# A gated mix of a Fourier convolution and a bilinear unit on one core: three Fourier stages on sums and differences of their inputs

## The chip, the core and the metric

The kernel runs on one core of a Trainium2 chip. The core's engines work side by side, each through its own queue in order: TensorE (PE) multiplies matrices, with its weight loads listed as PEld, VectorE (DVE) and ScalarE (ACT) work on tiles, GpSimd (POOL) and SyncE (SP) issue DMAs. Matmul results go to PSUM, here eight banks of 128 x 512 floats. The metric is the device time of one execution in microseconds; of several runs the median counts. The span is the stretch of the profiled execution from its first to its last instruction.

## What is computed

The input u has 2048 tokens and 512 channels. One branch convolves every channel with a kernel K of 2048 taps, which is itself made from 128 complex modes per channel; the other is a bilinear unit with hidden width 1792. A gate per token mixes them.

```python
P = jnp.exp((A * dt[:, None])[:, :, None] * pos[None, None, :])
K = 2.0 * jnp.einsum("dn,dnl->dl", C, P).real
Kf = jnp.fft.rfft(K, L2)
Uf = jnp.fft.rfft(u_t, L2)
y = jnp.fft.irfft(Uf * Kf[None, :, :], L2)[:, :, :L]
a = y.T + u * D_skip
b = ((x @ w_gate) * (x @ w_up)) @ w_down
g = sigmoid((u * gate_w).sum(-1))
out = g * a + (1 - g) * b
```

Here L2 is 4096, and x of the bilinear unit is read from u as well.

## The kernel before

**The order.** The kernel's work is written as tasks (`add`): an engine, an estimated time, what it reads and writes, a rank and, for some, an earliest time. `Work.run` then plays them on a clock of its own: it starts at each step the task that can start soonest, the lower rank first among equals, and emits the instructions in that order. On the chip only the resulting order of each engine's queue is left; nothing waits for the planner's clock.

**The bilinear unit (GLU).** The hidden width is cut into 14 tiles in five groups, and the tokens into four blocks of 512, which gives 56 calls of `hidden`, each of 24 matmuls for the gate (`pg`) and up (`pu`) products; `down` adds 672 more into `y`. Every float is split in a high and a low part (`xhi`, `xlo`, `whi`, `wlo`, `hh`, `hl`, `dhi`, `dlo`) and three products are summed, so the GLU is 2016 matmuls of 128x128 by 128x512. ScalarE makes the high parts and VectorE the low ones. Call number n of `hidden` may not start before `T_STEP * n - 5` on the planner's clock. GLU matmuls have rank 2, the highest number: Fourier work goes ahead of them where both can start. Group results are added into the output in DRAM by accumulating DMAs on GpSimd's queue (`out<-acc`); the last block of the last group is summed in the tile `kt` in `ends`.

**The tables and K.** For each of 16 blocks of 32 channels, `phases`, `amplitudes`, `direct_powers`, `leads`, `x_table` and `v_table` build two tables of powers, x (32 entries) and v (64 entries), on VectorE and ScalarE. `k_block` multiplies them on TensorE (`k<-v,x`) into one bank: 32 by 64 taps per channel. ScalarE copies that bank into `kt`, transposed, 32 elements apart. The last piece of a v table is the second `v<-v,sq` of its block.

**The Fourier transform.** A transform of 4096 points is done as a first stage over 64 points (`k_first` for K, in `u_part` for u), a second over 32 points (`m_second`), the product of the two spectra (`m_product`), an inverse (`m_inverse`) and a last stage (`m_last`). They run for four quarters q of 128 channels, each after the four blocks of K that it needs; a quarter's second stage is four tiles T. Between stages the data turn around in DRAM: `su_d` (u after its first stage), `sk_d` (K after its first), `y_d` (after the inverse). All these matmuls are in plain float32, in parts of the array (`tile_position`): u's first stage as two halves of 64 rows, the second stage as 64x32 tiles, the inverse as 32x64, the last as 128x64. The four small PSUM banks that they share are called `k`, as is K's own; so a Fourier batch reads `k<-in,w_t` (u's first or the last stage), `k<-kt,w1k_t` (K's first), `k<-in,w2s`, `k<-x,w2s` or `k<-v,w2s` (second) and `k<-y,w3s` (inverse). Batches of transforms are kept 6 us apart on the planner's clock (`APART`), in the last quarter 4 us (`LESS`). In the last quarter copies out of PSUM alternate between ScalarE and VectorE (`evict`).

## Time and profile before

| | before |
|---|---|
| median of 3 runs | 618.17 us (617.34 to 620.17) |
| span of the profiled execution | 615.6 us |
| instructions | 17,970 |
| granted TensorE clock, mean | 0.999 |
| PE / DVE / ACT / POOL busy | 605.5 / 514.9 / 420.1 / 88.6 us |
| moved by DMA | 121.67 MB, mean 198 GB/s |
| packets under 2 KB, of all | 66,548 of 103,238 |

A row of the profile's groups reads: line, engine, operation, tile written <- tiles read, shapes, count, then busy time and the mean of one in ns, then the idle time of the engine ahead of them and what ended it. All lines are L100 since one helper issues everything, so the tiles tell the groups apart. A row of the timeline has its start in us, the length of the stretch, the engine and the count. A float32 matmul stands twice in the trace, so `x128` there are 64 matmuls of the program. Recorded times of neighbours overlap by a few hundredths, on TensorE by more; the price of an instruction in a stream is the distance from start to start.

### The profile page before, as it was taken

What the parts mean: (1) busy time and instruction counts of PE and PEld (TensorE: products, weight loads), DVE (VectorE), ACT (ScalarE), POOL (GpSimd) and SP (SyncE); (2) the same over time, 40 slices, a digit from 0 to 9 for tenths busy, and PEclk for the clock granted to TensorE, in tenths of its full rate; (3) what the DMA queues carried; (4) which work ended last, traced back from release to release, by engine and by line L of the source; (5) the groups of instructions that cost most, each with busy time, mean ns of one, the idle gap of its engine ahead of it and who ended that gap; (6) DMA issues with size and microseconds to landing.
All of it is one profiled execution on the core that took longest, in us unless ns stands there. A gap on an engine that the chain in (4) does not pass through costs nothing.

```text
span 615.6 us, 17970 instructions
## 1 busy us (share of the span) xinstructions
PE 605.5 (98%) x7524; PEld 468.9 (76%) x7524; DVE 514.9 (84%) x810; ACT 420.1 (68%) x953; POOL 88.6 (14%) x125
## 2 busy tenths in 40 slices
PE   8999999999999999999999999999999999999996
PEld 5776777788777788887768888786888887678865
DVE  6958999999999999999889999999999842377342
ACT  5469877896878886679688768878885663533320
POOL 0211111111112201010120202021110101210120
PEclk9999999999999999999999999999999999999999
DMA  8795736555677977748797939787996789897771
GB/s 284 221 283 181 242 111 199 171 180 119 158 198 189 234 206 191 172 121 206 245 229 181 235 112 229 221 239 167 196 237 194 188 232 308 205 278 199 170 107 69
DMA packets 103238, 121.67 MB, mean 198 GB/s; under 512 B 6644, under 2 KB 66548, under 8 KB 102900
## 3 DMA queue, kind: packets, MB, share of 16 engines
q1 hardware_dynamic: 83732, 92.33, 49.3%
q0 software_dynamic: 19008, 28.06, 25.4%
q8 instruction: 59, 0.97, 0.6%
q14 instruction: 23, 0.19, 0.1%
q10 hardware_dynamic: 416, 0.13, 0.1%
HBM read 69.37 MB, written 51.12 MB: 196 GB/s over the span
## 4 chain that ended last, share of the span: by engine, by line
PE 75%; issue 10%; DMA 7%; DVE 4%; ACT 3%; POOL 1%; POOLq 0%; ACTq 0%; DVEq 0%
PE pg L100 20%; PE y L100 19%; PE pu L100 19%; PE k L100 18%; DMA out<-acc 3%; DMA raw<-in_xT 3%; ACT acc L100 1%; ACT ts L100 1%; DMA y<-in_xT 1%; DVE xlo L100 1%; POOL out L100 1%; ACT rt L100 1%; POOL su_d L100 1%; DVE v L100 1%; DVE t L100 1%
## 5 line engine op out<-in xcount | busy, mean ns | idle before, releaser
L100 POOL DMA_DIRECT2D out<-acc x60 | 51.3, 891 | 369.1 <-ACT acc L100 327.2
L100 PE MATMUL y<-dhi,hl 128*128 128x512 f32 x224 | 90.7, 405 | 1.5 <-ACT acc L100 0.9
L100 PE MATMUL pg<-xhi,wlo 128*128 128x512 f32 x224 | 90.3, 403 | 0.4 <-ACT h L100 0.3
L100 PE MATMUL pg<-xlo,whi 128*128 128x512 f32 x224 | 87.8, 392 | 1.6 <-issue 1.2
L100 PE MATMUL pu<-xhi,wlo 128*128 128x512 f32 x224 | 89.3, 399 | 0.0
L100 PE MATMUL pg<-xhi,whi 128*128 128x512 f32 x224 | 87.7, 392 | 0.5 <-ACT whi L100 0.5
L100 PE MATMUL y<-dhi,hh 128*128 128x512 f32 x224 | 87.5, 390 | 0.0
L100 PE MATMUL y<-dlo,hh 128*128 128x512 f32 x224 | 87.4, 390 | 0.0
L100 PE MATMUL pu<-xhi,whi 128*128 128x512 f32 x224 | 87.4, 390 | 0.0
L100 PE MATMUL pu<-xlo,whi 128*128 128x512 f32 x224 | 87.4, 390 | 0.0
L100 ACT ACTIVATE acc<-y,ngate 128x512 f32<-128x512 f32 x76 | 51.8, 692 | 29.9 <-PE y L100 18.4
L100 DVE TENSOR_TENSOR h<-pu,h 128x512 f32<-128x512 f32 x56 | 38.5, 688 | 39.7 <-PE pu L100 39.4
L100 ACT CAST hh<-h 128x512 fp32r<-128x512 f32 x56 | 34.9, 623 | 38.3 <-DVE h L100 38.2
L100 ACT COPY ts<-k 128x512 f32<-128x512 f32 (+1 forms) x112 | 47.7, 503 | 13.8 <-PE k L100 13.7
L100 PEld LDWEIGHTS y<-dhi,hl 128*128 128x128 f32 x224 | 42.0, 188 | 18.6 <-issue 2.7
L100 PEld LDWEIGHTS pg<-xhi,wlo 128*128 128x128 f32 x224 | 42.1, 188 | 18.1 <-issue 7.8
L100 ACT COPY h<-pg 128x512 f32<-128x512 f32 x56 | 32.9, 588 | 30.7 <-PE pg L100 24.5
L100 PEld LDWEIGHTS pu<-xhi,wlo 128*128 128x128 f32 x224 | 42.0, 188 | 12.7 <-issue 3.0
L100 PEld LDWEIGHTS pg<-xhi,whi 128*128 128x128 f32 x224 | 42.1, 188 | 12.5 <-ACT whi L100 2.1
L100 PEld LDWEIGHTS y<-dhi,hh 128*128 128x128 f32 x224 | 42.0, 188 | 9.3
L100 PEld LDWEIGHTS pu<-xhi,whi 128*128 128x128 f32 x224 | 42.2, 188 | 9.0
L100 PEld LDWEIGHTS pg<-xlo,whi 128*128 128x128 f32 x224 | 42.2, 188 | 8.8 <-DVE xlo L100 0.7
(109 smaller groups left out, 1169.5 us busy)
## 6 DMA issues: line engine op xcount, KB each, us to landing
raw<-in_xT SPq DMA_DIRECT2D x60, 256.0 KB, 4.6
out<-acc POOLq DMA_DIRECT2D x60, 256.0 KB, 6.7
raw<-in_wts SPq DMA_DIRECT2D x36, 256.0 KB, 4.4
su_d<-ts POOLq DMA_DIRECT2D x32, 256.0 KB, 4.6
y_d<-ts SPq DMA_DIRECT2D x16, 512.0 KB, 4.7
sk_d<-ts SPq DMA_DIRECT2D x14, 512.0 KB, 5.3
in<-sk_d SPq DMA_DIRECT2D x12, 512.0 KB, 6.8
in<-su_d SPq DMA_DIRECT2D x12, 512.0 KB, 5.4
```

What stands on the lines that cost most here:

```text
L100: got = getattr(self.engine, name)(*args, **kw)
```

## The change

The points of the transform are taken about the middle of the sequence. Tokens n1 and 63 - n1, and n2 and 31 - n2, are added and subtracted first, so cosines meet only sums and sines only differences, and each matrix has half its rows or columns:

- **u's first stage.** `u_part` now takes four columns of tokens at a time, four times instead of eight. VectorE makes two wide and four narrow sums and differences; then two batches of eight matmuls run in 32x64 tiles over 512 columns, where four matmuls in 64x128 halves ran per part. `su_d` is written in runs of 2 KB.
- **K.** Its powers lie in another order in v. ScalarE copies half of a bank into `kt` in reverse, and VectorE writes sum and difference of the halves. K's first stage has the same number of columns in one piece. `sk_d` is written in runs of 4 KB instead of 512 B.
- **The second stage** takes u and K side by side as 256 columns, in sixteen 32x32 tiles: 32 matmuls for both in a tile T, where 64 of 128 columns ran before. The product writes over its input tile.
- **The last stage** runs in 64x32 tiles on even and odd halves apart; ScalarE copies the odd half, VectorE adds and subtracts, and only then the gate multiplies. `y_d` is read in runs of 8 KB.
- **The steps**: `T_STEP` 9.85 instead of 10.3, and u's parts at 9, 29, 49 and 69 on the planner's clock instead of every 15.

```diff
-T_STEP = 10.3
+T_STEP = 9.85
+U_STEP = 20.0
...
-    def u_part(c):
...
+    def u_part(t):
+        ut = inp([P, 4, D])
+        rs = slice(4 * t, 4 * t + 4)
+        add("sp", 0.42, lambda: sp.dma_start(ut.t, uv[:, rs, :]), w=[ut], dma=1024, after=9.0 + U_STEP * t)
...
-        banks = [[bank() for _ in range(2)] for _ in range(2)]
-        sts = [stage([P, 2, D]) for _ in range(2)]
-
-        def fn():
-            for j in range(2):
-                for h in range(2):
-                    half = slice(64 * h, 64 * h + 64)
-                    pe.matmul(
-                        banks[j][h].t, w1_t[half], ut.t[half, j, :], start=True, stop=True, tile_position=(64 * h, 0)
-                    )
-
-        for j in range(2):
...
+        ones = [new("mid", "y", [P, 2, D], bufs=2) for _ in range(2)]
+        ops = (ALU.add, ALU.subtract)
+        for y, op in zip(ones, ops):
+            add(
+                "dve", 1.22,
+                lambda y=y, op=op: dve.tensor_tensor(out=y.t, in0=ut.t[:, :2], in1=ut.t[:, 2:], op=op), r=[ut], w=[y],
+            )
+        for s, op in enumerate(ops):
+            for d, y in enumerate(ones):
+                add(
+                    "dve", 0.69,
+                    lambda d=d, s=s, y=y, op=op: dve.tensor_tensor(
+                        out=ut.t[:, 2 * s + d], in0=y.t[:, 0], in1=y.t[:, 1], op=op
+                    ),
+                    r=[y], w=[(ut, 2 * s + d)],
+                )
+
+        def first(s):
+            banks, st = [bank() for _ in range(4)], new("mid", "ev", [P, KT, 4, P], bufs=2)
+
+            def fn():
+                for p in range(2):
+                    col, src = 64 * (p + s), 2 * s + (p + s) % 2
+                    for tq in range(4):
+                        lanes = slice(32 * tq, 32 * tq + 32)
+                        pe.matmul(
+                            banks[tq].t[64 * p : 64 * p + 64], w1_t.t[lanes, col : col + 64], ut.t[lanes, src],
+                            start=True, stop=True, tile_position=(32 * tq, 64 * p),
+                        )
+
+            add("pe", 1.08, fn, r=[(ut, 2 * s), (ut, 2 * s + 1), w1_t], w=banks, rank=1, hold=[st])
+            for tq in range(4):
+                add(
+                    "act", 0.59,
+                    lambda tq=tq: act.copy(st.t[:, :, tq], banks[tq].t.rearrange("p (f d) -> p f d", f=KT)),
+                    r=[banks[tq]], w=[(st, tq)],
+                )
...
+                        su_d[q, :, n0 : n0 + 4, :].rearrange("(t a) n d -> a t (n d)", a=4),
+                        st.t[:, q].rearrange("p n d -> p (n d)"),
...
-        for to, of, n in ((32, 0, 16), (56, 32, 8)):
+        for to, of, n in (((33, 64, 2), (0, 16, 1), 16), ((34, 64, 4), (33, 49, 2), 8)):
...
-            kts["now"] = new("tab", "kt", [P, 64, 32])
+            kts["now"] = new("tab", "kt", [P, 2, 2, 16, 32])
         kt, g0 = kts["now"], b % 4 * 8
         add("pe", 2.15, kgen, r=[x, v], w=[pk], rank=0, hold=[kt], many=work.APART)
-        add(
-            "act", 1.09,
-            lambda: act.copy(
-                kt.t[:, :, g0 : g0 + 8].rearrange("p n g -> p g n"), pk.t.rearrange("p (g j) -> p g j", j=64)
-            ),
-            r=[pk], w=[(kt, b % 4)],
-        )
+        pv = lambda a: pk.t.rearrange("p (g a b k) -> p g a b k", a=2, b=2, k=16)[:, :, a]
+        side = lambda h: kt.t[:, h, :, :, g0 : g0 + 8].rearrange("p b k g -> p g b k")
+        add("act", 0.6, lambda: act.copy(side(1), pv(0)[:, :, :, ::-1]), r=[pk], w=[(kt, (1, b % 4))])
+        for h, op in enumerate((ALU.add, ALU.subtract)):
+            add(
+                "dve", 0.45, lambda h=h, op=op: dve.tensor_tensor(out=side(h), in0=pv(1), in1=side(1), op=op),
+                r=[pk, (kt, (1, b % 4))], w=[(kt, (h, b % 4))], rank=0,
+            )
...
-                to = 0
-                for first, n, second in K_COLS[h]:
-                    for b in range(2):
-                        n0 = (first, second)[b]
-                        for c in range(4):
-                            lanes = slice(32 * c, 32 * c + 32)
-                            pe.matmul(
-                                banks[c].t[:, 32 * to : 32 * (to + n)], w1k_t[lanes, b],
-                                kt.t[lanes, n0 : n0 + n, :].rearrange("p n g -> p (n g)"),
-                                start=b == 0, stop=b == 1, tile_position=(32 * c, 0),
-                            )
-                    to += n
-
-            add("pe", 2.08, fn, r=[kt, m_w1k], w=banks, rank=-1, hold=sts, many=apart_of(q))
+                for b in range(2):
+                    for c in range(4):
+                        lanes = slice(32 * c, 32 * c + 32)
+                        pe.matmul(
+                            banks[c].t, w1k_t[lanes, b, 64 * h : 64 * h + P],
+                            kt.t[lanes, h, b].rearrange("p k g -> p (k g)"),
+                            start=b == 0, stop=b == 1, tile_position=(32 * c, 0),
+                        )
+
+            add("pe", 1.95, fn, r=[kt, m_w1k], w=banks, rank=-1, hold=sts, many=apart_of(q))
...
-                        sk_d[q, :, n0 : n0 + 8, :],
-                        st.t.rearrange("p n c g -> p n (c g)"),
+                        sk_d[q, :, n0 : n0 + 8, :].rearrange("(t a) n d -> a t (n d)", a=4),
+                        st.t.rearrange("p n c g -> p (n c g)"),
...
+            t, at = inp([P, 8, 2, P]), lambda: t.t
+            t = new("tab", "x", [P, 8, 2, P], bufs=2)
+                late["v"] = new("tab", "v", [P, 2, 8, 2, P])
+            t = late["v"]
...
-        banks = [[bank() for _ in range(2)] for _ in range(2)]
-        tos = [new("mid", "ev", [P, 2, 2, 2 * P], bufs=3) for _ in range(2)]
-            for which, (src, k) in enumerate(ins):
-                for part in range(2):
-                    for i in range(2):
-                        for j in range(4):
-                            for e in range(2):
-                                half = slice(64 * e, 64 * e + 64)
-                                c0 = 2 * P * part + P * i
-                                pe.matmul(
-                                    banks[which][e].t[32 * j : 32 * j + 32, c0 : c0 + P],
-                                    w.t[half, 4 * i + j, 32 * part : 32 * part + 32], src.t[half, k, 4 * i + j, :],
-                                    start=True, stop=True, tile_position=(64 * e, 32 * j),
-                                )
-
-        add("pe", 2.13, fn, r=[*ins, w], w=banks[0] + banks[1], rank=1, hold=tos, many=apart_of(q))
+        banks = [bank() for _ in range(4)]
+        to = new("mid", "ev", [P, 2, 2, 2, 2 * P], bufs=2)
+        at, parts = ins
+            src = at()
+            for f in range(8):
+                c, h = f % 4, f // 4
+                for r in range(4):
+                    lanes = slice(32 * r, 32 * r + 32)
+                    pe.matmul(
+                        banks[r].t[32 * c : 32 * c + 32, 2 * P * h : 2 * P * h + 2 * P], w.t[lanes, f],
+                        src[lanes, f].rearrange("p w d -> p (w d)"), start=True, stop=True,
+                        tile_position=(32 * r, 32 * c),
+                    )
+
+        add("pe", 1.15, fn, r=[*parts, w], w=banks, rank=1, hold=[to], many=apart_of(q))
...
-    def m_last(q, halves):
+    def m_last(q, gs):
...
+            for bs, t in zip(banks, src):
+                for tq in range(4):
+                    for p in range(2):
+                        lanes = slice(64 * p, 64 * p + 64)
+                        pe.matmul(
+                            bs[p].t[32 * tq : 32 * tq + 32], w4_t[lanes],
+                            t.t[lanes, 4 * tq : 4 * tq + 4].rearrange("p n d -> p (n d)"), start=True, stop=True,
+                            tile_position=(64 * p, 32 * tq),
+                        )
...
+            even, odd = banks[gs.index(g)]
+            cut = lambda x, n0=n0, n=n: x.t.rearrange("p (t s d) -> p t s d", t=2, s=2)[:, n0 : n0 + n]
+            side = lambda s1, fin=fin: fin.t[:, :, s1]
+            us = 0.15 + 0.27 * n
+            add("act", us - 0.1, lambda cut=cut, odd=odd, side=side: act.copy(side(1), cut(odd)), r=[odd], w=[(fin, 1)])
+            for s1, op in enumerate((ALU.add, ALU.subtract)):
+                add(
+                    "dve", us,
+                    lambda s1=s1, op=op, cut=cut, even=even, side=side: dve.tensor_tensor(
+                        out=side(s1), in0=cut(even), in1=side(1), op=op
+                    ),
+                    r=[even, (fin, 1)], w=[(fin, s1)], rank=0,
+                )
...
+            late["y"] = [new("tab", "x", [P, 16, P], bufs=2) for _ in range(2)]
+            for g in range(2):
+                for half in range(2):
+                    for p in range(2):
+                        lanes = slice(64 * p + 32 * half, 64 * p + 32 * half + 32)
+                        rows_y = y_d[q, 64 * half : 64 * half + 64].rearrange("(k p) n d -> p k (n d)", p=2)
+                        add(
+                            "sp", 0.42,
+                            lambda t=late["y"][g], lanes=lanes, rows_y=rows_y, p=p, g=g: sp.dma_start(
+                                t.t[lanes], rows_y[p, :, 16 * P * g : 16 * P * g + 16 * P]
+                            ),
+                            r=[(m_y, (q, 2 * half + k)) for k in range(2)], w=[(late["y"][g], (half, p))], dma=256,
```

The tables of sines and cosines change with it (`fourier_matrices`), as do the place of each token in the input and output arrays, the number of buffers of two tags (`in` and `ev`, three to two), and the gate's score, which now lies in the gate's own tile.

The change also moves instructions. On TensorE, this is the second stage of the last quarter in the kernel before; `pg`, `pu` and `y` are GLU matmuls:

```order
L100 MATMUL pu<-xlo,whi 128x512
L100 MATMUL pu<-xhi,whi 128x512
L100 MATMUL k<-v,w2s 32x128 x32
L100 MATMUL k<-x,w2s 32x128 x32
L100 MATMUL pu<-xhi,wlo 128x512
L100 MATMUL pu<-xlo,whi 128x512
```

And this is the whole of the last quarter behind K's first stage, in the changed kernel:

```order
L120 MATMUL y<-dlo,hh 128x512
L120 MATMUL y<-dhi,hh 128x512
L120 MATMUL k<-x,w2s 32x256 x64
L120 MATMUL k<-y,w3s 64x128 x64
L120 MATMUL k<-v,w2s 32x256 x64
L120 MATMUL k<-y,w3s 64x128 x64
L120 MATMUL k<-x,w_t 32x512 x16
L120 MATMUL y<-dhi,hl 128x512
```

Before, GLU matmuls stand between the batches, and 75 behind the last; now the batches follow each other and 18 GLU matmuls are behind them. Counted from the last block of K (`k<-v,x`), 357 of the 2016 GLU matmuls stood behind it, and now 108 do.

On VectorE, the end of the last v table in the kernel before:

```order
L100 TENSOR_TENSOR v<-v,sq 128x32x16
L100 TENSOR_TENSOR h<-pu,h 128x512
L100 SCALAR_TENSOR_TENSOR v<-v 128x32x8
L100 TENSOR_TENSOR v<-v,sq 128x32x8
L100 TENSOR_TENSOR hl<-h,hh 128x512
L100 TENSOR_TENSOR xlo<-raw,xhi 128x512 x2
```

and in the changed kernel:

```order
L120 TENSOR_TENSOR hl<-h,hh 128x512
L120 SCALAR_TENSOR_TENSOR v<-v 128x32x16
L120 TENSOR_TENSOR v<-v,sq 128x32x16
L120 SCALAR_TENSOR_TENSOR v<-v 128x32x8
L120 TENSOR_TENSOR xlo<-raw,xhi 128x512
L120 TENSOR_TENSOR v<-v,sq 128x32x8
L120 TENSOR_TENSOR kt<-k,kt 128x8x32 x2
```

Behind that table VectorE had 11 `xlo`, 10 `h` and 11 `hl` left; now it has none, three and three, and the sum and difference of K's last block (`kt<-k,kt`) come right behind the table.

Also on VectorE, the sums and differences of u's first part in the changed kernel (`y<-in`, `in<-y`), which the kernel before does not have:

```order
L120 TENSOR_TENSOR y<-in 128x1024
L120 TENSOR_TENSOR xlo<-raw,xhi 128x512
L120 TENSOR_TENSOR y<-in 128x1024
L120 TENSOR_TENSOR t<-v,turns 128x672
L120 TENSOR_TENSOR in<-y 128x512 x2
L120 TENSOR_TENSOR h<-pu,h 128x512
L120 TENSOR_TENSOR in<-y 128x512
L120 TENSOR_TENSOR xlo<-raw,xhi 128x512
```

They stand among the GLU's low parts and the tables, and u's matmuls wait for them.

More of the change, by code (lines that the diff above doesn't have):

```diff
@@ L351, in gated_mix_kernel @@
     pars = {}
-    gw = new("mid", "bd", [P, D])
+    gw = new("mid", "w3s", [P, D], bufs=2)
+    w1_t = new("mid", "w2s", [P, 192], bufs=2)
     def memsets():
@@ new lines, in u_part @@
+        for s, op in enumerate(ops):
[25 more added lines that the diff above has]
+                )
+            n0 = 16 * s + 4 * t
+            for q in range(KT):
```

346 lines of the change are left out of this document (173 added, 173 removed).

## The prediction

> **What bounds the kernel now.** I read the busy shares first, then one table of windows cut at the points where the Fourier work changes character, then TensorE's timeline at the end. In the windows each row gives the length, then PE, PEld, DVE, ACT and POOL busy, the clock, the DMA share and GB/s.
>
> ```profile
> PE 605.5 (98%) x7524; PEld 468.9 (76%) x7524; DVE 514.9 (84%) x810; ACT 420.1 (68%) x953; POOL 88.6 (14%) x125
> ...
> 0.00:60.00 60.00, 57.34 (x227) 40.67 (x228) 43.86 (x100) 38.92 (x98) 10.09 (x37) 1.00 0.77 244
> 60.00:494.20 434.20, 431.67 (x5900) 339.35 (x5906) 417.07 (x627) 338.52 (x773) 62.21 (x72) 1.00 0.74 192
> 494.20:535.30 41.10, 41.10 (x383) 30.22 (x367) 11.83 (x23) 20.13 (x47) 6.52 (x6) 1.00 0.91 252
> 535.30:589.75 54.45, 54.25 (x947) 43.64 (x946) 32.73 (x47) 20.11 (x34) 6.88 (x8) 1.00 0.90 210
> 589.75:615.60 25.85, 21.17 (x92) 14.98 (x91) 9.36 (x16) 2.42 (x4) 2.87 (x2) 0.99 0.41 78
> ```
>
> VectorE's 84% hides two stages. From 60 to 494.2 us it is busy 417.07 of 434.2 us, 96%: it builds the tables from which K is made, and that queue is full. From 494.2 on it is busy 53.9 of 121.4 us. TensorE is full throughout. So until the last table both engines bound the kernel together, and behind it TensorE alone does. This is TensorE behind that point:
>
> ```profile
> 501.11 2.07 PE L100 MATMUL k<-v,x 128*32 128x64 f32 x128
> ...
> 507.41 2.00 PE L100 MATMUL k<-kt,w1k_t 32*128 32x512 f32 x16
> ...
> 513.65 2.04 PE L100 MATMUL k<-kt,w1k_t 32*128 32x256 f32 x48
> ...
> 535.31 1.16 PE L100 MATMUL k<-v,w2s 64*32 64x128 f32 x64
> 536.21 1.22 PE L100 MATMUL k<-x,w2s 64*32 64x128 f32 x64
> ...
> 571.46 2.15 PE L100 MATMUL k<-y,w3s 32*64 32x128 f32 x128
> ...
> 589.75 3.65 PE L100 MATMUL k<-v,w_t 128*64 128x512 f32 x16
> ```
>
> The last block of K is made at 501.11, its first stage ends at about 515.65, the second stage of the last quarter starts at 535.31, its last stage at 589.75. That chain of 88.6 us is serial through VectorE and DRAM, and today GLU matmuls cover it: by the order 357 of the 2016 stand behind the last block of K.
>
> **The change on TensorE.** Prices are steps from the start of a batch to the start of what follows.
>
> ```profile
> 20.65 1.99 PE L100 MATMUL k<-in,w_t 64*128 64x512 f32 x8
> 22.56 0.50 PE L100 MATMUL pu<-xhi,wlo 128*128 128x512 f32 x1
> ...
> 223.71 2.11 PE L100 MATMUL k<-in,w2s 64*32 64x128 f32 x128
> 225.75 0.50 PE L100 MATMUL y<-dhi,hl 128*128 128x512 f32 x1
> ...
> 309.82 2.79 PE L100 MATMUL k<-in,w_t 128*64 128x512 f32 x12
> 312.44 1.03 PE L100 MATMUL k<-y,w_t 128*64 128x512 f32 x4
> 313.40 0.50 PE L100 MATMUL pg<-xhi,wlo 128*128 128x512 f32 x1
> ...
> 246.65 0.39 PE L100 MATMUL pu<-xhi,wlo 128*128 128x512 f32 x1
> ...
> 248.46 0.39 PE L100 MATMUL pu<-xhi,whi 128*128 128x512 f32 x1
> 248.78 2.10 PE L100 MATMUL k<-y,w3s 32*64 32x128 f32 x128
> 250.81 0.50 PE L100 MATMUL pu<-xhi,wlo 128*128 128x512 f32 x1
> ```
>
> A batch of u takes 1.91 us, a second stage 2.04, a last stage 3.58; a GLU matmul 0.226 (eight steps in 1.81). The inverse batch runs in tiles of 32x64, eight at once: 128 records of 128 columns in 2.03 us, 16,384 columns. u's new batch uses the same tiles with half those columns: 1.0 us. The last stage of a quarter has the same columns: 2.0. The second stage halves its columns only if sixteen 32x32 tiles run at once, which no row shows: between 1.0 (they do) and 2.0 (eight do). I take 1.0, since 64-row and 32-row tiles both reached eight. Saved: 8 x 0.9 + 16 x 1.0 + 4 x 1.6 = 29.6 us in all, and 8 x 0.9 + 12 x 1.0 + 2 x 1.6 = 22.4 ahead of the last block of K. K's first stage keeps its columns; the saving there is nothing or a few hundredths, within the bounds below.
>
> But the order also moves 249 GLU matmuls ahead of that block (357 behind it become 108), 56.3 us. TensorE therefore cannot be there before 501.1 + 56.3 - 22.4 = **535 us**.
>
> **The change on VectorE.** The table's last piece today, the three groups of GLU work that still stand behind it (window from 494.2), those of the same kind ahead of it (from 60), and the prices:
>
> ```profile
> 493.81 0.42 DVE L100 TENSOR_TENSOR v<-v,sq 128x256 f32<-128x256 f32 x1
> ...
> L100 DVE TENSOR_TENSOR hl<-h,hh 128x512 fp32r<-128x512 f32 x11 | 7.6, 692 | 6.2 <-ACT hh L100 6.2
> L100 DVE TENSOR_TENSOR xlo<-raw,xhi 128x512 fp32r<-128x512 f32 x11 | 7.4, 690 | 6.7 <-ACT xhi L100 6.7
> L100 DVE TENSOR_TENSOR h<-pu,h 128x512 f32<-128x512 f32 x10 | 6.9, 691 | 31.0 <-PE pu L100 31.0
> ...
> L100 DVE TENSOR_TENSOR h<-pu,h 128x512 f32<-128x512 f32 x40 | 27.5, 688 | 5.0 <-PE pu L100 4.7
> ...
> L100 DVE TENSOR_TENSOR y<-ev 128x1024 f32<-128x1024 f32 x16 | 19.5, 1221 | 3.8 <-ACT ev L100 3.3
> L100 DVE TENSOR_TENSOR y<-y,bd 128x512 f32<-128x512 f32 x32 | 20.6, 682 | 0.1
> L100 DVE COPY ts<-k 128x256 f32<-128x256 f32 x4 | 1.4, 418 | 3.4 <-PE k L100 3.4
> ```
>
> Back to back, 512 columns cost 20.6/32 = 0.64 us, 1024 cost 1.22, 256 cost 0.42. New ahead of the last table: u's eight wide and sixteen narrow sums and differences, 8 x 1.22 + 16 x 0.64 = 20.1; two per block of K for 15 blocks, 30 x 0.42 = 12.6; the last stages of two quarters, 8 x 0.64 = 5.1. Moved there: of the 32 GLU operations behind it six stay, so 26/32 of 21.9 us, 17.8. Together 55.6 us. What can hide it is VectorE's idle time: 16.1 us before 60 (some 5 of it before any data are there) and 17.1 after, of which 5.0 waited for TensorE. At most 16 can be filled, at least none; I take 12. The table then ends at 494.2 + 55.6 - 12 = 538 us.
>
> One price has no row: the new K operations write at a stride of 32 elements. ScalarE's copy into the same tile shows such a stride beside a plain one:
>
> ```profile
> L100 ACT COPY kt<-k 128x512 f32<-128x512 f32 x16 | 18.0, 1127 | 15.4 <-PE k L100 15.3
> ...
> L100 ACT COPY ts<-k 128x512 f32<-128x512 f32 x60 | 31.8, 595 | 8.2 <-PE k L100 8.2
> ```
>
> That is 1.04 ns more per element, 0.27 us per 256 columns. VectorE pays nothing, or as much: 0 to 8 us on 30 operations. I take 4, midway, because the engine differs: **542 us**, later than TensorE's 535, so TensorE waits there. The Trainium skill speaks against the cheap end: by Advanced Engine Details and Errata, section Memory Cachelines, accesses that each fall in a new 16-byte line of SBUF are slowed. ScalarE's row agrees with it; by the rule the sum would be 4 us longer.
>
> ScalarE loses half of its strided copy per block and gains eight copies of 0.6 us; at 68% it covers both. u's matmuls now wait for six VectorE operations, 5.0 us a quarter, with GLU matmuls queued behind them; the order puts 135 GLU matmuls first, which covers the first quarter. If that cover fails, 5 us go there once.
>
> **The exposed end.** From the last block of K to the end of its first stage the order has the same two groups of 18 GLU matmuls: 14.5 us, as today. Then come 54 GLU matmuls and a last stage, 14.2 us; today the second stage starts 19.7 us after, behind the DRAM round trip. Between 14.2 and 19.7 I take 17, since K is now written in runs of 4 KB and not of 512 B. From there no GLU matmul stands between the steps (18 are left at the very end, and they wait for the last quarter's sums). The chain is 1.0 (second stage), 10.5 on VectorE (two tiles: four copies at 0.64, two products of 2 x 1.22 + 2 x 0.64, 0.5 for the real column), 2.0 inverse, 1.3 copies, 1.0, 10.0 and 2.0, 1.3 again, then out to DRAM and back:
>
> ```profile
> y_d<-ts SPq DMA_DIRECT2D x16, 512.0 KB, 4.7
> v<-y_d SPq DMA_DIRECT2D x4, 512.0 KB, 5.7
> ...
> 592.72 2.87 POOL L100 DMA_DIRECT2D out<-ts x2 [4.62 <-DVE ts L100]
> ...
> out<-ts POOLq DMA_DIRECT2D x1, 256.0 KB, 7.5
> out<-ts POOLq DMA_DIRECT2D x7, 512.0 KB, 9.8
> ```
>
> 1.0 + 10.5 + 2.0 + 1.3 + 1.0 + 10.0 + 2.0 + 1.3 + 4.7 + 5.7 = 39.5, say 40 to the start of the last stage (36 to 44). Behind it: today the accumulating DMA is issued 3.0 us after that start and lands 7.5 to 9.8 later; now two sums or differences and a multiplication stand between, so 15 (11.4 to 17). Sum: 542 + 14.5 + 17 + 40 + 15 = 628.5 us against this execution's 615.6. The runs' median, 618.17, is 2.6 above that span; **predicted 631 us, slower**.
>
> **The rivals.** *VectorE absorbs its additions* (0.14): the point is the last block of K. If the table is there by 535, TensorE's floor decides: 535 + 14.5 + 14.2 + 36 + 11.4 = 611, measured 614, faster by 0.7%. For it speaks that 33 us of idle time lie ahead of that point; against it that only about 16 can be filled. *The whole saving arrives* (0.04): 615.6 - 29.6 = 586, measured 589. It needs GLU matmuls to cover the chain, and the order has left it 18. *Eight tiles, not sixteen* (0.10): twelve second stages a microsecond longer put TensorE at 547 and the chain at 42: 636, measured 638. *The end runs cold* (0.18): with TensorE idle for most of the last 55 us the granted clock, 1.00 or 0.99 in every window now, could fall to half, doubling 7 us of matmuls on the chain and the 4 us of GLU at its end, less what the DMA beside it hides; with VectorE's stride at its full price, 546 + 14.5 + 17 + 47 + 18 = 642.5, measured 645. The Trainium skill's TensorE: Matmul & The Clock Gate, Part 1, says that idle gaps above some 3.4 us bring the half rate; no row here has such a gap late in the run, so the trace can't tell.
>
> **How the numbers follow.** My forecast has 0.54; its own bounds give 619 to 645. About 0.5%, 3 us, is what a measurement can tell from no change: faster is below 615.1, slower above 621.3. Of the forecast's 0.54, 0.02 fall below and 0.09 between; of the absorbing case 0.11 and 0.03. Faster 0.11 + 0.04 + 0.02 = 0.17, same 0.12, slower 0.71. The range 614 to 650 leaves out the full saving and the far ends.
>
> **What would show it.** Right: the last k<-v,x batch at 537 to 550 us with a wait for VectorE's v or kt ahead of it; u's batches at 1.0 us and second stages of 1.0; TensorE idle for over 20 us behind the last 54 GLU matmuls; VectorE above 95% until then. Wrong: that batch at 535 or earlier, or a second stage starting within 14 us of the first stage's end with the whole rest done in 47.

## The result, and the profile after

The changed kernel takes 833.34 us (824.24 to 834.05 in four runs) where the one before takes 617.75 us in the same runs: **34% slower**, ratio 1.343 with a 95% interval of 1.336 to 1.351. The direction was forecast; the time lies 183 us above the top of the range.

The busy shares of the changed kernel, and the TensorE clock and the DMA engines' share in 40 slices:

```profile
span 832.0 us, 15999 instructions
PE 627.5 (75%) x6500; PEld 465.7 (56%) x6500; DVE 565.7 (68%) x883; ACT 429.1 (52%) x964; POOL 87.1 (10%) x125
...
PEclk9998989999998999857998999759889999765557
DMA  8677646365664955423938655327548754327555
```

TensorE was 98% busy and is 75% busy; VectorE, which the forecast made the bound, 68%. In the first 36 slices the clock digit falls to 7 or less six times, and the DMA digit there is 2 or 3. The waits for DMAs in this kernel read: engine and tile that waited, what it waited for, microseconds in all, times, the longest.

```profile
PE k L120 <- DMA in<-y_d: 90.0, 6, 19.5
ACT whi L120 <- DMA raw<-in_wts: 51.4, 5, 35.5
ACT xhi L120 <- DMA raw<-in_xT: 34.9, 13, 7.6
ACT ts L120 <- DMA sk_d<-ts: 30.1, 1, 30.1
PEld k L120 <- DMA in<-y_d: 20.5, 1, 20.5
ACT ev L120 <- DMA su_d<-ev: 11.5, 2, 6.3
```

The last block of K, forecast at 542, stands at 692.05 us. Three of these transfers have a new shape (`in<-y_d`, `sk_d<-ts`, `su_d<-ev`); the loads into `raw` are as before, and the engines wait for them longer. In the kernel before, no engine has such a row for `y_d`, `sk_d<-ts` or `su_d`, nor `whi` one for `raw`, and that of `xhi` reads:

```profile
ACT xhi L100 <- DMA raw<-in_xT: 11.8, 11, 1.8
```

A last stage on TensorE's timeline, with what ended the idle time in brackets, and a window over another one (length, PE, PEld, DVE, ACT, POOL busy, clock, DMA share, GB/s):

```profile
360.06 1.96 PE L120 MATMUL k<-in,w_t 64*32 64x512 f32 x16 [15.45 <-DMA in<-y_d]
380.71 2.08 PE L120 MATMUL k<-in,w_t 64*32 64x512 f32 x16 [18.69 <-DMA in<-y_d]
...
538.40:561.00 22.60, 3.71 (x32) 0.62 (x32) 0.02 (x1) 1.19 (x3) 0.00 (x0) 0.50 0.23 69
```

The last stage was priced at 2.0 us and takes 22.6 from the start of its first half to the end of its second. Each half waits for one transfer of 1 MB, here 15.45 us (ahead of the 22.6) and 18.69. The other engines stand nearly still as well, the clock is at half, and the DMA engines are 23% busy. So the data are slow to come while the DMA engines as a group have room. This is the row of the queue before and after, whose bytes are nearly the same:

```profile
q1 hardware_dynamic: 83732, 92.33, 49.3%
...
q1 hardware_dynamic: 80672, 90.31, 35.6%
```

The first row is that of before (packets, MB, share of 16 engines' time), the second that of after. This queue's packets take no more of the engines' time than before: 49.3% of 615.6 us is 303 us, 35.6% of 832.0 us is 296 us. The engines' work in it did not grow, though the kernel took a third longer. That most of them were idle while a few were busy is what the experiments are to show.

### The profile page after: what moved, and what is told of

It reads as the page before. It is cut to its first block, busy times and chain, and to the rows that moved or that the text cites. A ratio compares the mean times of both kernels' runs of the same rounds, so it can differ in the third digit from the quotient of the medians.

```text
span 832.0 us, 15999 instructions
## 1 busy us (share of the span) xinstructions
PE 627.5 (75%) x6500; PEld 465.7 (56%) x6500; DVE 565.7 (68%) x883; ACT 429.1 (52%) x964; POOL 87.1 (10%) x125
## 3 DMA queue, kind: packets, MB, share of 16 engines
q1 hardware_dynamic: 80672, 90.31, 35.6%
## 5 line engine op out<-in xcount | busy, mean ns | idle before, releaser
L120 PE MATMUL y<-dhi,hl 128*128 128x512 f32 x224 | 96.3, 430 | 33.9 <-DVE hl L120 18.4
L120 PE MATMUL y<-dlo,hh 128*128 128x512 f32 x224 | 91.6, 409 | 0.0
L120 PE MATMUL y<-dhi,hh 128*128 128x512 f32 x224 | 91.2, 407 | 0.0
L120 ACT COPY ts<-k 128x256 f32<-128x256 f32 (+1 forms) x89 | 35.9, 470 | 86.0 <-PE k L120 44.4
L120 PE MATMUL k<-in,w_t 64*32 64x512 f32 x96 | 11.4, 980 | 90.0 <-DMA in<-y_d 90.0
L120 ACT COPY ev<-k 128x512 f32<-128x512 f32 x88 | 46.7, 597 | 47.5 <-PE k L120 30.7
L120 DVE TENSOR_TENSOR ts<-k,ts 128x512 f32<-128x512 f32 (+1 forms) x18 | 10.6, 625 | 84.1 <-ACT ts L120 84.0
L120 DVE TENSOR_TENSOR hl<-h,hh 128x512 fp32r<-128x512 f32 x56 | 38.4, 686 | 39.1 <-ACT hh L120 38.9
L120 DVE TENSOR_TENSOR xlo<-raw,xhi 128x512 fp32r<-128x512 f32 x60 | 40.7, 688 | 31.4 <-ACT xhi L120 31.3
L120 ACT CAST hh<-h 128x512 fp32r<-128x512 f32 x56 | 34.9, 623 | 47.7 <-DVE h L120 47.7
L120 PEld LDWEIGHTS pu<-xhi,wlo 128*128 128x128 f32 x224 | 43.1, 192 | 26.3 <-DVE h L120 10.6
L120 ACT CAST xhi<-raw 128x512 fp32r<-128x512 f32 x60 | 36.4, 623 | 35.5 <-DMA raw<-in_xT 34.9
## 6 DMA issues: line engine op xcount, KB each, us to landing
su_d<-ev POOLq DMA_DIRECT2D x32, 256.0 KB, 11.4
```

The costliest lines, as they stand in the source:

```text
L120: got = getattr(self.engine, name)(*args, **kw)
```

## The experiments

**One cause, three transfers.** Theory T1: the new access patterns begin with a dimension of 2 (`y_d`) or 4 (`su_d`, `sk_d`), and such a transfer is spread over only so many of the 16 DMA engines. The first kernel times the disputed transfers by themselves. It leaves the whole computation out.

```diff
+    for case in (load_whole, load_pairs, load_halves, write_rows, write_fours, write_quarters, one_su, each_su, fourth_su):
+        for _ in range(3):
+            case(t)
+            nc.vector.memset(t, 0.0)
```

> Leaves the whole computation out: it times the disputed transfers one at a time, each three times, with a memset on VectorE between any two, so that the gaps between the memsets show each transfer from issue to landing. Loads of 1 MB from y_d: whole (128 rows), with the outermost dimension of 2 as the changed kernel has them, and as two halves of 64 partitions; writes of 512 KB to sk_d: by rows as before, with the outermost dimension of 4 as changed, and as four quarters of 32 partitions; writes of 256 KB to su_d from the software queue: one with the outermost dimension of 4, four such one after the other, and four of 32 partitions each. T1: pairs 5 to 8 times as long as whole (20 us or more against some 5), fours 2 to 4 times as long as rows, one of the su writes near 11 us, halves and quarters within 2 us of whole and rows. Rival B (length of the runs): pairs like halves and fours like quarters.

VectorE's timeline: the gap in brackets ahead of each memset is one case, a transfer or the parts into which it is cut, from the end of the memset before it to the last landing. First the load of 1 MB whole and as pairs and as two halves, then the write to `sk_d` by rows, in fours and in four quarters, then to `su_d` one, four of the changed kind, and four cut by partitions.

```profile
33.19 1.76 DVE L72 MEMSET t<- 128x2048 f32 x1 [5.51 <-DMA t<-y_d]
...
89.70 1.76 DVE L72 MEMSET t<- 128x2048 f32 x1 [22.65 <-DMA t<-y_d]
...
133.14 1.76 DVE L72 MEMSET t<- 128x2048 f32 x1 [7.74 <-DMA t<-y_d]
...
152.59 1.76 DVE L72 MEMSET t<- 128x2048 f32 x1 [3.19 <-DMA sk_d<-t]
...
182.39 1.76 DVE L72 MEMSET t<- 128x2048 f32 x1 [10.63 <-DMA sk_d<-t]
...
206.48 1.76 DVE L72 MEMSET t<- 128x2048 f32 x1 [4.15 <-DMA sk_d<-t]
...
231.78 1.76 DVE L72 MEMSET t<- 128x2048 f32 x1 [7.78 <-DMA su_d<-t]
...
269.28 1.76 DVE L72 MEMSET t<- 128x2048 f32 x1 [12.51 <-DMA su_d<-t]
...
301.01 1.76 DVE L72 MEMSET t<- 128x2048 f32 x1 [7.16 <-DMA su_d<-t]
```

The same megabyte takes 5.5 us whole and 22.65 in pairs, 4.1 times as long; cut into two transfers of 64 partitions it takes 7.7, although every run of data has the same length and address as in the pairs. That rules out rival B (the length of the runs). The factor is below the 5 to 8 expected, since issue and landing are in both. The writes to `sk_d` show 3.2, 10.6 and 4.15 us. Two sizes were missed: the halves are 2.2 us behind the whole and not within 2, and one write to `su_d` takes 7.8 us here, not near 11. Windows inside three of the gaps (VectorE, POOL, clock, DMA share, GB/s):

```profile
27.67:33.19 5.52, 0.01 (x1) 0.00 (x0) 1.00 0.57 190
67.04:89.70 22.66, 0.01 (x2) 0.00 (x0) 1.00 0.11 46
...
171.75:182.39 10.64, 0.01 (x2) 0.00 (x0) 1.00 0.17 49
```

While the pairs are under way, and nothing else is, the 16 engines are 11% busy: two of 16 busy would be 12.5%. For the fours it is 17%, where four engines all the time would be 25%; the start and the landing are part of the 10.6 us. The single packets in this trace show it directly: in the pairs' 22.66 us, exactly two packets are under way at once for 19.98 us and never more than three; in the fours, four are under way for 5.45 of 10.64 us and never more than six; in the whole load, 14 or more for 2.9 of 5.52 us. From the first packet to the last the pairs take 20.5 us and the whole load 3.7, a factor of 5.5. By the Trainium skill, DMA: Bandwidth & Descriptors, section Why a DMA increments its semaphore by 16 and not by 1, the number of engines is the largest up to 16 that divides the slowest dimension of both access patterns, so 2 and 4 here; these shares and counts agree.

Then the changed kernel with the transfers cut so that each begins with 32 or 64 rows. The order of the other work is the same in all four: TensorE, VectorE and ScalarE run the same instructions in the same order as in the changed kernel. With the writes to `su_d` cut this way, its later loads wait for all four writes of each part.

```diff
-                        t.t, y_d[q].rearrange("(k p) n d -> p k (n d)", p=2)[:, :, 16 * P * g : 16 * P * g + 16 * P]
+                    rows_y = y_d[q].rearrange("(k p) n d -> p k (n d)", p=2)
+                    for p in range(2):
+                        sp.dma_start(
+                            t.t[64 * p : 64 * p + 64], rows_y[p, :, 16 * P * g : 16 * P * g + 16 * P]
+                        )
...
-                        sk_d[q, :, n0 : n0 + 8, :].rearrange("(t a) n d -> a t (n d)", a=4),
-                        st.t.rearrange("p n c g -> p (n c g)"),
+                    rows_k = sk_d[q, :, n0 : n0 + 8, :].rearrange("(t a) n d -> a t (n d)", a=4)
+                    for a in range(4):
+                        lanes = slice(32 * a, 32 * a + 32)
+                        sp.dma_start(rows_k[a], st.t[lanes].rearrange("p n c g -> p (n c g)"))
...
-                        su_d[q, :, n0 : n0 + 4, :].rearrange("(t a) n d -> a t (n d)", a=4),
-                        st.t[:, q].rearrange("p n d -> p (n d)"),
+                        su_d[:, :, n0 : n0 + 4, :].rearrange("f (t a) n d -> a t f (n d)", a=4)[a],
+                        st.t[32 * a : 32 * a + 32].rearrange("p f n d -> p f (n d)"),
```

The load of `y_d` alone:

> Only the load of the third stage's rows from y_d is changed: each of its six transfers of 1 MB, whose access pattern starts with a dimension of 2, is issued as two of 64 partitions, each with an outermost dimension of 64. T1 (a transfer with few outermost rows is spread over few of the DMA engines): the three last stages of a quarter fall from 22.7 us to the predicted 2.0, their 20 us waits in front go, and so does the share of these loads in the slowness of others; 95 to 130 us saved, time 705 to 740. Rival A (VectorE bounds the kernel as in the prediction and the loads are only the last thing waited for): the wait moves to another release, at most 30 us saved, 800 or more. Rival B (the many short runs of 64 floats to a partition make the load slow whatever its outermost dimension): unchanged, 830 to 840.

The writes to `sk_d` alone:

> Only the writes of K's first stage to sk_d are changed: each transfer with an outermost dimension of 4 is issued as four of 32 partitions. T1: the waits of the stage before the last ones for sk_d and the waits for a free staging tile (30 us at ScalarE) go, but the loads of y_d stay; 20 to 45 us saved, time 790 to 815. Rival A: four times as many issues at the same place, 833 to 845. Rival B: unchanged, 830 to 840.

The writes to `su_d` alone:

> Only the writes of u's first stage to su_d are changed: the same number of transfers of the same size, cut by the quarter of the partitions rather than by the quarter of the columns, so that the outermost dimension is 32 and not 4; the later loads wait for all of them. T1: landing falls from the median of 11.4 us to 5 or 6, the eviction's waits of 11.5 us go, and the stages of the first quarter start earlier; 15 to 45 us saved, time 790 to 820. Rival A: 830 to 840. Rival B: unchanged landings of 11 us, 830 to 840.

All three:

> All three: the loads of y_d by halves, the writes to sk_d by quarters of the partitions, the writes to su_d by quarters of the partitions. T1: no transfer is held to a few DMA engines, so what is left is what the prediction worked out: VectorE carries the middle, its last table at 542, and the tail stands exposed, 631 (620 to 650). If the prediction's VectorE bound was wrong and the saving arrives: 589 to 605. Rival A or B (something else than the spread over engines slows the kernel): 760 or more.

| | median, us | saved against 833.34 |
|---|---|---|
| `y_d` | 729.07 | 104.3 |
| `sk_d` | 772.26 | 61.1 |
| `su_d` | 807.45 | 25.9 |
| all three | 641.80 | 191.5 |

The three savings add up to 191.2 us, and together they bring 191.5. (The runs of one kernel lie up to 11 us apart here, so that the two agree within 1 us is luck; that they agree within a few per cent is not.) T1 stands for the three transfers, and rivals A and B fall; what T1 says of VectorE is taken up below. The size for `sk_d` was missed: 61.1 us against 20 to 45. The waits point to the reason. This is what is left of ScalarE's waits with only `sk_d` mended:

```profile
ACT whi L120 <- DMA raw<-in_wts: 43.8, 5, 35.3
ACT xhi L120 <- DMA raw<-in_xT: 12.0, 13, 2.4
...
ACT dhi L120 <- DMA raw<-in_wts: 1.6, 2, 0.8
```

`xhi` fell from 34.9 to 12.0 us and `dhi` from 19.0 to 1.6: the GLU's own loads, which nobody had touched, had been standing in the same queue behind K's writes. In the changed kernel, for instance, SyncE issues two writes to `sk_d` from 242.23 us on and two loads into `raw` from 248.18 on, and a cast waits for such a load until 262.20, while these loads land in 4.6 us at the median in the kernel before:

```profile
262.20 0.62 ACT L120 CAST xhi<-raw 128x512 fp32r<-128x512 f32 x1 [7.40 <-DMA raw<-in_xT]
```

With all three mended the row of `xhi` reads 13.0, near the 11.8 of before, and that of `whi`:

```profile
ACT whi L120 <- DMA raw<-in_wts: 1.2, 2, 1.0
```

Against the kernel before, the mended one has the ratio 1.039 (1.036 to 1.042): what was forecast is tested on it below.

**VectorE or TensorE, and the exposed end.** The mended kernel still leaves 108 GLU matmuls behind the last block of K. A larger `T_STEP` paces the GLU later.

```diff
-T_STEP = 9.85
+T_STEP = 10.3
```

> The kernel with all three transfers cut, and T_STEP 10.3 (as before the change) instead of 9.85: 192 GLU matmuls stand behind the last block of K, not 108. Theory E (the end is a serial chain of about 90 us from the last block of K on, so the time is that block's time plus 90, as long as TensorE's own work behind it is shorter): TensorE may be there at 549.6 - 84 x 0.235 = 530, VectorE with 6 us of GLU operations less at 532 to 544; take 538: 630 us (624 to 636). Rival F (VectorE holds the last block where it is, at 549): 640. Rival G (once the end is covered the whole saving on TensorE arrives): 595 to 610.

> As step_103 with T_STEP 10.9: 279 GLU matmuls behind the last block. E: TensorE there at 509, VectorE at 525 to 537, take 531; chain and TensorE's work behind it both near 88: 620 us (613 to 627). F: 640. G: 595 to 605.

> As step_103 with T_STEP 11.2: 300 GLU matmuls behind the last block. E: VectorE at 524 to 536, take 530; behind it 300 x 0.235 + 20 = 90 us on TensorE: 621 us (613 to 628). F: 640. G: 595 to 605.

> As step_103 with T_STEP 11.6: 393 GLU matmuls behind the last block. E: VectorE at 517 to 529, take 525; behind it TensorE's own work, 393 x 0.235 + 20 = 112 us, is longer than the chain: 638 us (629 to 643), with TensorE idle ahead of the blocks of K. F: 640 or more. G: 595 to 605.

(The letters of the theories are defined anew in each group of kernels.) All four miss, on the slow side. Pacing the GLU later does not bring the block of K forward (its place is that of the profiled execution):

| | GLU matmuls behind the last block | that block at, us | median, us |
|---|---|---|---|
| all_split (9.85) | 108 | 549.60 | 641.80 |
| step_103 | 192 | 548.65 | 653.02 |
| step_109 | 279 | 554.12 | 671.48 |
| step_112 | 300 | 553.20 | 672.37 |
| step_116 | 393 | 555.83 | 692.84 |

F named the place of the block rightly within 7 us, yet its time of 640 was wrong, since the work moved behind the block still has to be done there. In step_116 TensorE stands idle for 56 of the 555.8 us ahead of the block, most of it waiting for the low parts of its own GLU work (in the row, all of the kernel's waits of this kind):

```profile
PE y L120 <- DVE hl L120: 52.0, 24, 5.0
```

The same row of all_split has 5.1 us. Is that VectorE's amount of work? The next kernels leave out, on VectorE, u's 24 sums and differences and K's 32; the matmuls read the halves unsummed (K's first stage only the half that ScalarE copies). The order of TensorE and ScalarE stays the same.

```diff
-                lambda y=y, op=op: dve.tensor_tensor(out=y.t, in0=ut.t[:, :2], in1=ut.t[:, 2:], op=op), r=[ut], w=[y],
+                lambda: None, r=[ut], w=[y],
...
-                "dve", 0.45, lambda h=h, op=op: dve.tensor_tensor(out=side(h), in0=pv(1), in1=side(1), op=op),
+                "dve", 0.45, lambda: None,
...
-                            kt.t[lanes, h, b].rearrange("p k g -> p (k g)"),
+                            kt.t[lanes, 1, b].rearrange("p k g -> p (k g)"),
```

> all_split with the sums and differences of u's first stage (24 operations) and of K's blocks (32) left out on VectorE; the matmuls read the unsummed halves, everything else and the order of the other work stay. That takes 9.7 + 10.2 + 30 x 0.675 = 40 us from VectorE ahead of the last block of K. F (with T_STEP 9.85 TensorE and VectorE both arrive at the last block near 549): TensorE's own work holds it there, gain at most the waits, 634 to 641 us. G (VectorE alone was the bound): table 30 to 40 us earlier, 600 to 612.

> As lean_985 with T_STEP 10.3 (192 GLU matmuls behind the last block): F (there VectorE was late): the block falls from 548.65 to TensorE's floor of 530 to 534, and the 100 us behind it stay: 633 to 640 us against 653. Rival H (the finer interleaving itself costs it: TensorE waits on GLU operations in VectorE's queue in any case): 648 to 655.

> As lean_985 with T_STEP 10.9 (279 behind): F: TensorE's floor at the last block 509, VectorE 549 - 40 = 509 and some idle: block at 509 to 522, the 108 us behind it as in step_109: 618 to 632 us against 671. H: 660 to 672.

They take 640.91, 641.34 and 663.35 us. Here are the last block of K on TensorE and the end of its table on VectorE, first of lean_985, then of all_split:

```profile
549.69 2.07 PE L120 MATMUL k<-v,x 128*32 128x64 f32 x128
548.56 0.62 DVE L120 TENSOR_TENSOR v<-v,sq 128x256 f32<-128x256 f32 x1 [1.51 <-ACT sq L120]
...
549.60 2.07 PE L120 MATMUL k<-v,x 128*32 128x64 f32 x128
548.48 0.62 DVE L120 TENSOR_TENSOR v<-v,sq 128x256 f32<-128x256 f32 x1 [1.11 <-ACT sq L120]
```

The operations left out were priced at 40 us; VectorE's busy time ahead of the block fell by 32.4 us (520.7 to 488.3), and the block did not move. With the order of the change **TensorE's queue alone** is enough to hold it there, as F says. VectorE's table ends no earlier either, in part since its queue has GLU operations in it that wait for TensorE's products; this row is of lean_985, then of all_split:

```profile
DVE h L120 <- PE pu L120: 13.0, 22, 2.5
...
DVE h L120 <- PE pu L120: 3.4, 7, 1.6
```

So the place where an engine's work ends does not tell whether that engine sets it. With `T_STEP` 10.3 the gain is 11.7 us, between F (13 to 20) and H (up to 5); the block comes at 539.80, short of F's 530 to 534. With 10.9 the gain is only 8.1 of the 39 to 53 that F gave, and the block comes at 551.66. There H is the better account: TensorE waits for single GLU operations, and less work on VectorE does not shorten these waits. The row of step_109, then that of lean_109:

```profile
PE y L120 <- DVE hl L120: 27.9, 16, 3.6
...
PE y L120 <- DVE hl L120: 28.0, 17, 2.9
```

So the order was changed in another way: the planner counts VectorE's operations at less than their cost, and its order puts the tables further ahead.

```diff
+        us *= 0.93 if engine == "dve" else 1.0
         task = Task(len(self.tasks), engine, us, fn, rank, after, dma)
```

> All three transfers cut; the planner counts VectorE's operations at 0.96 of their cost, so that its order puts the tables earlier and 273 GLU matmuls behind the last block of K instead of 108. F (VectorE bounds it once TensorE's work is moved behind): TensorE's floor at the last block 511, VectorE 509 us of work and 10 to 29 idle ahead of it: 519 to 538, and 90 to 95 behind: 620 us (611 to 635). G (the exposed end was all): block at 511, 606. H (the order stalls TensorE on VectorE's GLU operations, as with T_STEP): 640 or more.

> As plan_96 with 0.93: 336 GLU matmuls behind the last block. F: VectorE 504 and idle, block at 514 to 533, behind it 336 x 0.235 + 20 = 99 us on TensorE: 623 us (613 to 634). G: 496 + 99 = 596. H: 640 or more.

> As plan_96 with 0.9 and T_STEP 10.3: 360 behind the last block. F: VectorE 503 and idle, 513 to 532, behind it 105 us: 627 us (618 to 638). G: 490 + 105 = 597. H: 640 or more.

> The order of plan_93 (336 GLU matmuls behind the last block of K) with the 56 sums and differences of u's first stage and of K's blocks left out on VectorE, as in lean_985: 40 us less there ahead of the last block. F (VectorE's amount of work holds plan_93 at 640): the last block comes 25 to 35 us earlier, 603 to 618. H (the order of single operations, not their sum, makes TensorE wait): at most 10 us gained, 629 to 641.

| | GLU matmuls behind the last block | that block at, us | median, us |
|---|---|---|---|
| plan_96 | 273 | 528.13 | 640.38 |
| plan_93 | 336 | 522.49 | 640.55 |
| plan_90 | 360 | 535.27 | 653.75 |
| lean_plan_93 | 336 | 507.38 | 624.96 |

(A single run of plan_93's kernel once more took 641.9.) In plan_96 and plan_93 the block does come earlier now, by 21 and 27 us, to where F put it, but the time is H's 640: what is behind the block grows from all_split's 90.6 us to 106.9 and 115.7, where F had 90 to 95 and 99. The windows of plan_93 ahead of the block and behind it (length, then TensorE's busy time):

```profile
0.00:522.49 522.49, 494.64 (x5429) 372.10 (x5429) 507.04 (x794) 386.30 (x884) 66.77 (x110) 0.99 0.74 185
522.49:638.20 115.71, 103.59 (x1073) 75.21 (x1072) 55.40 (x90) 38.60 (x79) 16.14 (x16) 0.96 0.85 196
```

TensorE is idle for 27.9 us ahead of the block and 12.1 behind it; in all_split it is 12.5 and 29.2. What the cover saves at the end, waits ahead of the block take back: 40.0 us in all against 41.7. In plan_90 the block comes later than F's 532, and the time is longer. With VectorE's 56 operations left out of plan_93's order, the block comes 15.1 us earlier still and the time falls by 15.6. F expected 25 to 35 and H at most 10; neither is right alone. With the tables put early VectorE's new operations hold part of it. That the rest is the order of the single operations is likely, but no run shows it: leaving the operations out takes away both their time and TensorE's waits for them. No version here is faster than the kernel before; the one at 625 us leaves work out.

## Why the prediction was wrong

**The step that failed is a term that the sum does not have.** Every new sum, matmul and matmul order was priced, and no transfer was priced by its new shape: the last stage's 2.0 us takes it for granted that the data are there, and the last quarter's round trip (4.7 + 5.7) is taken from rows of the kernel before. The one place that speaks of a new shape, "Between 14.2 and 19.7 I take 17, since K is now written in runs of 4 KB and not of 512 B", reads the diff's longer runs as a gain. The longer runs were real, the outermost dimension was not looked at: writing `"(t a) n d -> a t (n d)"` with a of 4 and `"(k p) n d -> p k (n d)"` with p of 2 took 128 rows apart into 4 or 2 groups. That costs 191.5 of the 215.6 us lost. The change itself has the better form in one place: in the last quarter it reads `y_d` into `x`, in pieces of 32 partitions. TensorE's group for that stage in the changed kernel, with the idle time ahead of it behind the bar:

```profile
L120 PE MATMUL k<-x,w_t 64*32 64x512 f32 x32 | 5.0, 1025 | 9.5 <-issue 9.5
```

It stands 9.5 us for the last copies and a round trip through DRAM that the forecast put at 10.4. The six waits of up to 19.5 us are those of the first three quarters.

**The rest of the forecast is tested by the kernel with the three transfers cut**, 641.8 us for 631 forecast and inside its own range. Its windows, cut at 60 us, the last block of K, the last quarter's second stage and its last stage:

```profile
0.00:60.00 60.00, 57.08 (x264) 41.25 (x265) 53.46 (x116) 42.07 (x94) 7.69 (x37) 1.00 0.79 259
60.00:549.60 489.60, 480.05 (x5393) 370.15 (x5392) 467.27 (x699) 365.04 (x821) 67.52 (x82) 1.00 0.73 178
549.60:580.50 30.90, 30.52 (x290) 20.66 (x292) 11.22 (x21) 13.90 (x35) 3.29 (x3) 1.00 0.98 250
580.50:619.50 39.00, 20.17 (x513) 12.62 (x513) 22.95 (x31) 6.44 (x12) 1.57 (x1) 0.61 0.77 181
619.50:640.20 20.70, 10.68 (x50) 5.43 (x50) 8.76 (x17) 1.23 (x3) 2.88 (x2) 0.75 0.55 110
```

| step | forecast | all_split |
|---|---|---|
| last block of K, us from the start | 542, by VectorE | 549.6, by TensorE |
| from there to the last quarter's second stage | 14.5 + 17 | 30.9 |
| to its last stage | 40 | 39.0 |
| to the end | 15 | 20.7 |
| span | 628.5 | 640.2 |

- **The exposed end** was right in mechanism and place: 90.6 us against 86.5. The end itself is 5.7 us longer than the 15 it was given (11.4 to 17). TensorE's last 18 matmuls wait for the last sums, as the prediction has them do:

```profile
619.51 4.52 PE L120 MATMUL k<-x,w_t 64*32 64x512 f32 x32 [9.30 <-issue]
629.64 0.79 PE L120 MATMUL y<-dhi,hl 128*128 128x512 f32 x1 [5.62 <-DVE kt L120]
```

- **VectorE** was near its price, and its role was wrong. K's strided operations cost the upper bound:

```profile
L120 DVE TENSOR_TENSOR kt<-k,kt 128x256 f32<-128x256 f32 x32 | 21.6, 675 | 3.3 <-ACT kt L120 3.3
```

  That is 0.675 us against 0.42 plain, 7.7 us on 30 operations and not the 4 taken; and of the 33 us that VectorE was idle ahead of that point before, some 4 were filled (28.9 are left) and not 12. The Trainium skill's section Memory Cachelines, cited there, had spoken for that end, and the trace agrees. (These operations also read at a stride; no run separates the two.) The last table ends at 549.10, 7 us behind the forecast and 0.50 ahead of the block. But TensorE does not wait there: the wait for `v` or `kt` that the prediction names as its sign is missing, VectorE is busy for 53.46 + 467.27 = 520.73 of the 549.6 us, and in lean_985 the block stays where it is with 32.4 us less on VectorE. So nothing supports 542 as a time that VectorE sets; whether VectorE alone would have held the block there too, no run shows. That 542 lies near the measured place is luck: TensorE's term, which decides, was put at 535.
- **TensorE's floor** was put at 535 and is 549.6. Three terms were too small. A second stage takes 1.42 us from its start to that of the next matmul, and not 1.0:

```profile
351.06 1.50 PE L120 MATMUL k<-in,w2s 32*32 32x256 f32 x64
352.48 0.50 PE L120 MATMUL y<-dhi,hl 128*128 128x512 f32 x1
```

  The records of one batch do start in groups of 16, which fits sixteen tiles at once, as taken; but behind the first two groups they start 16.7 ns apart, and the GLU matmul starts 304 ns behind the last. Twelve batches at 0.42 more are 5.0 us. Two last stages took 3.0 and 3.3 instead of 2.0, 2.3 us in all; the third, behind the block, took 1.88, so their matmuls were priced rightly and stood still within the batch. And the 249 moved GLU matmuls took 63.8 us (summed from start to start, 458.6 for 1908 against 394.8 for 1659), 7.5 more than at 0.226. Most of that is waiting: TensorE's idle time ahead of the block grew from 5.2 us to 12.5, with 4.9 of it for VectorE's `hl` and 3.1 for `v`. Together 14.8, for a difference of 14.6.
- **The rivals.** "The end runs cold" has its place right: the clock is 0.61 in the 39 us before the last stage. Its reason is another one. The clock falls to half at about 589 us, 21 us before TensorE's wait of 9.30 us begins, and the longest gap of the last quarter up to there is 2.46:

```profile
587.23 0.40 PE L120 MATMUL k<-y,w3s 32*64 32x128 f32 x2 [2.46 <-DVE y L120]
...
590.00:595.00 5.00, 3.07 (x95) 2.00 (x81) 3.19 (x5) 0.51 (x2) 0.00 (x0) 0.50 0.76 265
```

  By the Trainium skill's Part 1, cited there, gaps above some 3.4 us bring the half rate. The changed kernel's long waits agree with it (in the window 538.40:561.00 TensorE waits 18.89 us, at a clock of 0.50); this fall, behind shorter gaps, it does not account for. The rival gave 645 for a kernel that takes 641.8 once mended, but from other terms: 47 us where 39.0 were measured, and a block at 546 that VectorE's stride puts there. "VectorE absorbs its additions" was right that TensorE decides the place of the block, and gave 614, since it used the floor of 535 and a table that is there by then. "Eight tiles, not sixteen", which needs 2.0 us for a second stage, is refuted by the 1.42, "the whole saving arrives" by every kernel here.

What stays open is whether an order exists that covers the end without making TensorE wait on VectorE in the middle. Eight were tried, four of them also without VectorE's new work, and none did.

## What to carry to other kernels

Price a transfer whose access pattern is rewritten, even where bytes and rows stay the same: read the outermost dimension first, and put the partitions there (with 32 rows or more outermost the transfers here were fast, with 2 or 4 slow). In a profile, a slow load while the DMA share is low and all else stands still points to it, and so do waits for other loads that nobody changed. Take work off an engine before calling it the bound: here 32 us less on an engine that was 95% busy, and whose work ended half a microsecond ahead of the block, changed the time by 0.9 us.

## What was not expected of the hardware

- Two transfers by halves of the partitions moved the megabyte in 7.7 us, 2.9 times as fast as one in pairs (22.65), with the same runs of data.
- One write of 256 KB from the software queue with 4 outermost rows took 7.78 us and four in a row 12.5: they run beside each other, and still slower than the four cut by partitions, 7.2 in all.
- The losses of the three slow transfers added up (191.2 us one by one, 191.5 together, with runs up to 11 us apart), though two of the three share a queue and the loads of others wait behind them.
- The clock fell to half, and stayed there for 34 us, while no gap on TensorE up to there was longer than 2.46 us in the last quarter; TensorE had only small tiles to work on. Whether the small tiles are the cause is not shown.
